# Gate lists of two tokens across the partitions, in a fused Fourier-mixing and expert-lookup kernel

## The chip, the cores and the metric

The kernel runs on one core of one Trainium2 chip. The core's engines are TensorE (PE in the profile, its weight loads PEld), VectorE (DVE), ScalarE (ACT), GpSimd (POOL) and SyncE (SP, which here only issues DMAs). Each runs its own instructions strictly in the order in which they stand; semaphores tie the engines together. The metric is the device time of one execution in microseconds, the median of the runs shown.

## The reference, cut to what matters

```python
xn  = layernorm(x)                                  # 2048 tokens x 512
y   = Real(DFT_seq(DFT_hid(xn)))                    # FNet mixing, as matrices given as inputs
q   = xn @ w_q                                      # 32 heads, 2 x 128
s1, s2 = q1 @ k1.T, q2 @ k2.T                       # 64 keys each
# of each head the two best sums s1[i]+s2[j]: expert index e = 64*i + j, gate g = softmax
act = gelu(sum_d xn[n,d] * u[e,d])                  # 4096 experts
out = sum over heads, k of  g * act * v[e]
result = x + y + out
```

A token has 64 (head, k) entries, each an expert index `e` in 0..4095 and a gate `g`. The kernel computes the gelu for all 4096 experts of a block of 128 tokens with matmuls, and multiplies it by a dense gate matrix that it builds from the lists.

## The kernel before, in words

First comes the Fourier part with the layer norm (to about 90 us of the trace), then the score part (to about 443 us), then the expert part (to the end).

**Score part.** The heads are in 8 chunks (`NCH`), the tokens in 16 tiles of 128. Step n = 16 j + i makes the scores of chunk j and tile i: 12 PE matmuls (`scores`, L799), one ACT eviction (L804), and DVE's MAX8 and FIND_INDEX8 (L807, L811). `routing` turns the top entries into list fields of tile `z`; its small operations go partly to POOL (`ge`). Beside this run preparations of the next chunk's weights (`m_prep`), of the expert tables (`fill_uv`, `fill_far`), and `compare` units: the kernel exploits the symmetry of the DFT matrices, and a `compare` unit loads a piece of those matrices (512 KB) and checks the symmetry. `EARLY` lists the units that run here, at the steps in `at_k`; their loads are issued three steps earlier, the differences are POOL operations (L755, L761), and ACT judges them two steps later (L781). They share three `cx` buffers.

**Expert part.** It works on 14 blocks b of 128 tokens. `u_part(b, cg)`, cg = 0..7, makes the gelu inputs: 48 PE matmuls of 128x128 each (L959), then an ACT gelu (L962). `g_mm(b, tg)` builds the dense gates of 32 tokens: for each 16 tokens DVE writes `L`, a one-hot of the low 7 bits of `e` (128 list entries on the partitions, 16 x 128 columns, L983); for 32 tokens it writes `R`, a one-hot of the high 5 bits (L991), multiplied by the gate (L994). One PE matmul for each token multiplies `L` (weights) with `R` (32 columns) into PSUM tile `g` (L996). The gate is split into a high and a low f16 half, so the 64 entries of a token fill 128 partitions. There are two `L` and two `R` buffers, and two `g` tiles (tag `pg`) of two PSUM banks. `w_part(b, tg)` multiplies `g` by the gelu in place (DVE L1007), ACT makes the f16 high half (L1012) and DVE the low half (L1015, "the subtraction" below); after L1015 the `g` tile is free. `v_part(b, pv, cg)` makes the output: 12 PE matmuls of 128x512 each (L1024), and `finish` adds the rest (L1039) and stores.

PE's order is fixed. In a steady state: the output of block b (cg 0 to 3), `g_mm(b+1, 2)`, the output (cg 4 to 7), `g_mm(b+1, 3)`, `u_part(b+2, 0..3)`, `g_mm(b+2, 0)`, `u_part(b+2, 4..7)`, `g_mm(b+2, 1)`, and on. `g_mm(b, t)` needs the `g` tile that the subtraction two quarters earlier frees.

The lists come to the partitions through `compact`: PE transposes (L698) and one ACT copy (L699) that writes each value twice.

The last two of the 16 token tiles (256 tokens) aren't in blocks. They are done as rows: 128 gathers of u and v rows by POOL (`fetch`, L1050, `BUFS` buffers), a DVE dot product (`dot`, L1066), ACT gelu and scaling (`gain`, L1076 to L1079), and a POOL addition (L1084). `pick` spreads these over the expert part. In the same way `paced` spreads the other `compare` units (`compare`, `compare_r` for rows 0, `compare_w` for the hidden matrix W; here on DVE) and `fit` units, and `after(k, f)` runs f k turns later. `verdict` reduces all checks to flags at cg 4 of the last block.

A scheduler sorts each engine's instructions when the program is built; `follow` and `hold` only bind that order and add no wait on the chip.

Of the kernel before, what the change touches and what calls it, by code (L numbers as in the profile page):

```python
# [10 lines left out]
F16 = mybir.dt.float16  # L11
# [25 lines left out]
def tile_fnet_peer(ctx, tc, x, ca, cb, c5, wt, wf, wr, wq, kt, ut, vn, uv, out):  # L37
# [14 lines left out]
    z_d = dram.tile([NT, P, 3 * P], F16, name="z_d")  # L52
# [40 lines left out]
    EARLY = [*range(8, 24), *range(40, 52)]  # L93
# [462 lines left out]
    def part_b(safe, stS, stP, stE, xt, u_sb, cmp_p):  # L556
# [55 lines left out]
        z = sp.tile([P, NT, 3, 2, 2, H], F16, name="z")  # L612
# [17 lines left out]
        def routing(part, j, vals, idx, t0=0, t1=NT, ge=nc.gpsimd):  # L630
# [20 lines left out]
            elif part == 1:  # L651
# [5 lines left out]
                nc.vector.tensor_copy(zi[:, :, 2, :, 0, hs], g)  # L657
                if not safe and t1 == NT:
                    nc.gpsimd.tensor_copy(gts[:, :, :, hs], g[:, n - NS:])
                nc.vector.tensor_tensor(zi[:, :, 2, :, 1, hs], g, zi[:, :, 2, :, 0, hs], op=ALU.subtract)  # L660
            else:
# [25 lines left out]
                for l in range(2):  # L687
                    for w, v in enumerate((lc, e)):
                        ge.tensor_copy(zi[:, :, w, :, l, hs], v)
# [3 lines left out]
        def compact(b, src, pool, tag):  # L693

            cmp = pool.tile([P, 3, P, 2], F16, tag=tag, name=f"cmp{b}")
            p = pc(f"zt{b}", F16) if b < 2 else psum.tile([P, 512], F16, tag="pb", name=f"zt{b}", bufs=2)
            for w in range(3):
                nc.tensor.transpose(p[:, w * P:(w + 1) * P], src[:, w], ident16)  # L698
            nc.scalar.activation(cmp, p[:, :3 * P].rearrange("p (w n) -> p w n", w=3).unsqueeze(3)  # L699
                                 .to_broadcast([P, 3, P, 2]), AF.Copy)  # L700
            CMP[b] = cmp
# [154 lines left out]
        at_k = [7, 10, *(16 * j + i for j in range(1, 7) for i in (0, 4, 7, 9) if (j, i) != (2, 0)), 112, 122, 125]  # L856
# [8 lines left out]
        for j in range(NCH):  # L865
# [8 lines left out]
            for i in range(NT):  # L874
# [20 lines left out]
                if j + 1 == NCH and i == NT - 1:  # L895
                    for b in range(2):
                        compact(b, z[:, b].rearrange("p w k t h -> p w (k t h)"), cmp_p, f"cmp{b}")
                    nc.sync.dma_start(z_d[2:4].rearrange("i p f -> p i f"),
                                      z[:, 2:4].rearrange("p i a k t h -> p i (a k t h)"))
# [6 lines left out]
        for part in range(3):  # L906
            routing(part, *pend, 4, NT, nc.vector)
        nc.sync.dma_start(z_d[4:].rearrange("i p f -> p i f"),
                          z[:, 4:].rearrange("p i a k t h -> p i (a k t h)"))
# [7 lines left out]
        RS = [lr.tile([P, 32, NC], F16, name=f"R{k}") for k in range(2)]  # L917
# [16 lines left out]
        BUFS = 6  # L934
# [10 lines left out]
        def compact_d(b):  # L945
            zb = bp.tile([P, 3, P], F16, tag="zb", name=f"zb{b}", bufs=1)
# [27 lines left out]
        def g_mm(b, tg, after=None):  # L974
            cmp = CMP[b]
            p = pg(f"g{b}_{tg}")
            def bc(w, t0, t1, n):
                return cmp[:, w, tg * TG + t0:tg * TG + t1, :].unsqueeze(2).to_broadcast([P, t1 - t0, n // 2, 2])

            for hf in range(2):  # L980
                LS.append(LS.pop(0))
                L = LS[-1]
                nc.vector.tensor_tensor(  # L983
                    L.rearrange("p t (l two) -> p t l two", two=2),
                    io_lam.rearrange("p (l two) -> p l two", two=2).unsqueeze(1).to_broadcast([P, 16, P // 2, 2]),
                    bc(0, hf * 16, hf * 16 + 16, P), op=ALU.is_equal)
                if hf == 0:
                    RS.append(RS.pop(0))
                    R = RS[-1]
                    Rv = R.rearrange("p t (c two) -> p t c two", two=2)  # L990
                    nc.vector.tensor_tensor(  # L991
                        Rv, io_c.rearrange("p (c two) -> p c two", two=2).unsqueeze(1)
                        .to_broadcast([P, TG, NC // 2, 2]), bc(1, 0, TG, NC), op=ALU.is_equal)
                    nc.vector.tensor_tensor(Rv, Rv, bc(2, 0, TG, NC), op=ALU.mult)  # L994
                for t in range(16):
                    i = nc.tensor.matmul(p[:, hf, t * NC:(t + 1) * NC], L[:, t, :], R[:, hf * 16 + t, :],  # L996
                                         start=True, stop=True)
                    if after is not None:
                        follow(i.ins, after)
# [109 lines left out]
        def compare_r(n):  # L1109
# [14 lines left out]
            def work():  # L1124
                for ri, odd, e in cls:
                    sgn = (((1, 1, 1), (-1, 1, -1)), ((-1, -1, 1), (1, -1, -1)))[ri][odd]
                    f = (-1 if ri else 1) * sgn[1] * sgn[2]
                    m = ALU.add if ri else ALU.subtract
                    nc.vector.tensor_tensor(tv[e, 1], tv[e, 1], tv[e, 0], op=ALU.subtract if sgn[0] > 0 else ALU.add)
                    nc.vector.tensor_tensor(tv[e, 3], tv[e, 3], tv[e, 2], op=ALU.subtract if f > 0 else ALU.add)  # L1130
                    nc.vector.tensor_tensor(t[e, 0::2, 2:4], t[e, 0::2, 2:4], t[e, 0::2, 0:2], op=m)
                    if odd and ri:
                        nc.vector.tensor_copy(t[e, 2, 0:2], t[e, 0, 0:2])
                    elif odd == ri:
                        nc.vector.memset(t[e, 2, 0:2], 0.0)
                after(2, lambda: nc.scalar.activation(tf[:, P:], tf[:, P:], AF.Abs, accum_out=chk[:, n:n + 1]))

            after(2, work)
# [354 lines left out]
```

## Time and profile before

| | |
|---|---|
| median of 3 runs | 1112.83 us (1112.5 to 1113.57) |
| profiled execution | 1110.31 us, of it 1108.5 us from the first to the last instruction |
| PE busy | 1070.5 us (97%) |
| DVE busy | 963.9 us (87%) |
| ACT busy | 717.3 us (65%) |
| POOL busy | 595.4 us (54%) |

The busy time of an engine is the union of its instructions. A time behind `<-` in brackets is idle time of the engine just before a row, and who ended it. Groups of rows show the shape written and read, the count, the busy time and the mean duration. The durations of consecutive DVE instructions overlap a little; what one costs is the distance from its start to the next start.

### The profile page before, as it was taken

How to read it: one execution, taken by the hardware profiler on the slowest of the kernel's cores; microseconds unless marked ns; L12 is line 12 of the kernel's file. 1: busy time of each engine (PE TensorE's matmuls, PEld its weight loads, DVE VectorE, ACT ScalarE, POOL GpSimd, SP SyncE). 2: the span in 40 equal slices, each digit the busy share in tenths (PEclk: the TensorE clock that was granted, in tenths of full speed). 3: DMA queues.
4: the chain of work that ended last, by engine and by line, in shares of the span. 5: the costliest groups of instructions: out<-in, count | busy, mean ns of one | idle time of the engine just before them, and what ended most of it. 6: DMA issues, size and time to landing. Idle time of an engine off the chain costs nothing. (4 is left out here: it accounts for less than half of the span.)

```text
span 1108.5 us, 28483 instructions
## 1 busy us (share of the span) xinstructions
PE 1070.5 (97%) x11070; PEld 696.6 (63%) x11070; DVE 963.9 (87%) x2748; ACT 717.3 (65%) x1326; POOL 595.4 (54%) x553
## 2 busy tenths in 40 slices
PE   5899999999999999999989999999999999999987
PEld 4355555454544544987675967858667696776933
DVE  6879897979999999987999798999998889998971
ACT  3566657778788767533756766668666776767650
POOL 0013537588797846211646575665575656556431
PEclk9799999999999999999999999999999999999999
DMA  8248153435445331463568667766876667666511
GB/s 326 84 168 288 39 210 99 174 130 208 152 153 197 110 123 65 152 212 92 183 189 248 193 206 244 223 220 191 242 232 214 209 204 252 222 200 200 166 29 51
DMA packets 84936, 196.78 MB, mean 178 GB/s; under 512 B 10770, under 2 KB 27559, under 8 KB 84792
## 3 DMA queue, kind: packets, MB, share of 16 engines
q1 hardware_dynamic: 63898, 123.55, 33.0%
q0 software_dynamic: 20736, 71.31, 21.7%
q8 instruction: 88, 1.44, 0.5%
q14 instruction: 56, 0.46, 0.1%
q10 hardware_dynamic: 158, 0.01, 0.0%
HBM read 177.74 MB, written 17.10 MB: 176 GB/s over the span
## 5 line engine op out<-in xcount | busy, mean ns | idle before, releaser
L799 PE MATMUL s<-m,xq 128*128 128x512 f16 x1536 | 338.9, 379 | 0.0
L959 PE MATMUL z<-xb,u 128*128 128x128 f16 x5376 | 306.4, 220 | 0.0
L959 PEld LDWEIGHTS <-u 128*128 128x128 f16 x5376 | 302.1, 98 | 0.0
L1024 PE MATMUL v<-v,act 128*128 128x512 f16 x1344 | 300.2, 382 | 1.6 <-DVE act L1015 1.6
L1084 POOL TENSOR_TENSOR ov<-ov,ga 128x512 f32<-128x512 f32 x128 | 176.9, 1382 | 206.9 <-ACT ga L1079 173.4
L799 PEld LDWEIGHTS <-xq 128*128 128x128 f16 x1536 | 148.3, 98 | 171.3 <-issue 0.2
L1024 PEld LDWEIGHTS <-act 128*128 128x128 f16 x1344 | 129.6, 98 | 153.2 <-issue 4.5
L983 DVE TENSOR_TENSOR L<-io_lam,cmp 128x2048 f16<-128x2048 f16 x112 | 154.7, 1405 | 31.2 <-PE g L996 31.1
L1050 POOL DMA_INDIRECT ga<-in_uv_dram,eix x128 | 153.4, 1198 | 48.1 <-POOL ov L1084 36.9
L807 DVE MAX8 vals<-ss 128x8 f32<-128x64 f32 x1024 | 152.5, 216 | 14.0 <-ACT ss L804 14.0
L962 ACT ACTIVATE act<-z,scl 128x512 f32<-128x512 f32 x112 | 76.1, 681 | 93.6 <-PE z L959 92.9
L811 DVE FIND_INDEX8 idx<-vals,ss 128x8 uint16<-128x256 f32 x256 | 107.1, 419 | 0.0
L804 ACT ACTIVATE ss<-s,wsc 128x512 f32<-128x512 f32 x112 | 75.5, 680 | 43.1 <-PE s L799 33.8
L1079 ACT ACTIVATE ga<-ga,za 128x512 f32<-128x512 f32 x128 | 92.3, 722 | 10.2 <-ACT za L1077 0.4
L781 ACT ACTIVATE cx<-cx 128x896 f32<-128x896 f32 x64 | 60.6, 947 | 48.7 <-DVE cx L761 36.3
L1066 DVE SCALAR_TENSOR_TENSOR ga<-ga,px 128x512 f32<-128x512 f32 x128 | 85.7, 676 | 0.2
L1012 ACT ACTIVATE act<-g 128x1024 f16<-128x1024 f32 x56 | 73.2, 1308 | 18.2 <-DVE g L1007 18.2
L1007 DVE SCALAR_TENSOR_TENSOR g<-act,scl,g 128x1024 f32<-128x1024 f32 x56 | 71.6, 1279 | 10.7 <-ACT act L962 6.6
L1015 DVE TENSOR_TENSOR act<-g,act 128x1024 f16<-128x1024 f32 x56 | 72.7, 1298 | 6.6 <-ACT act L1012 6.5
L169 POOL TENSOR_TENSOR wq<-wq,wh 128x1024 f16<-128x1024 f32 x26 | 55.5, 2136 | 24.2 <-ACT wq L166 23.7
L996 PE MATMUL g<-R,L 128*128 128x32 f16 x1792 | 53.8, 176 | 13.0 <-DVE act L1015 12.5
L996 PEld LDWEIGHTS <-L 128*128 128x128 f16 x1792 | 51.6, 96 | 21.7 <-DVE act L1015 8.7
(281 smaller groups left out, 1298.4 us busy)
## 6 DMA issues: line engine op xcount, KB each, us to landing
cx<-in_cb_dram SPq DMA_DIRECT2D x50, 448.0 KB
wq<-in_wq_dram SPq DMA_DIRECT2D x32, 512.0 KB
fit<-in_wq_dram SPq DMA_DIRECT2D x28, 512.0 KB
uv<-in_ut_dram SPq DMA_DIRECT2D x16, 512.0 KB
uv<-in_vn_dram SPq DMA_DIRECT2D x16, 512.0 KB
cx<-in_cb_dram SPq DMA_DIRECT2D x28, 224.0 KB
xq<-in_x_dram SPq DMA_DIRECT2D x8, 512.0 KB
xt_d<-xq SPq DMA_DIRECT2D x16, 256.0 KB
```

Of the source, the lines that this page charges most:

```text
L799: mm = nc.tensor.matmul(ps, xt[i][:, l, kd, :], m[:, r, kd, :], start=(n == 0), stop=(n == 3 * KD - 1))
L807: nc.vector.max(vals[:, i, w, :, h], s[:, g, :])
L811: nc.vector.max_index(idx[:, i, w].rearrange("p k h -> p (k h)"), vals[:, i, w, 0:2].rearrange("p k h -> p (k h)"), s[:, w * HC:g + 1, :]. ...
L959: mm = nc.tensor.matmul(p[:, cc * P:(cc + 1) * P], ug[:, l, c % 2, kd, :], xb[:, r, kd, :], start=(n == 0), stop=(n == 3 * KD - 1))
L962: GL[mm.ins.name] = nc.scalar.activation(act[:, cg * 4:cg * 4 + 4, :].rearrange("p c n -> p (c n)"), p, AF.Gelu_apprx_tanh, scale=zsc)
L983: nc.vector.tensor_tensor(L.rearrange("p t (l two) -> p t l two", two=2), io_lam.rearrange("p (l two) -> p l two", two=2).unsqueeze(1).to_ ...
L996: i = nc.tensor.matmul(p[:, hf, t * NC:(t + 1) * NC], L[:, t, :], R[:, hf * 16 + t, :], start=True, stop=True)
L1024: mm = nc.tensor.matmul(pv, w16[:, c, :, l], vg[:, r, c % 2, :], start=(c == 0 and k == 0), stop=(c == NC - 1 and k == 2))
L1050: nc.gpsimd.indirect_dma_start(out=t, out_offset=None, in_=uv, in_offset=bass.IndirectOffsetOnAxis(ap=eix[:, n].rearrange("p k h -> p (k h ...
L1066: nc.vector.scalar_tensor_tensor(t, t, 1.0, T["x"], op0=ALU.mult, op1=ALU.mult, accum_out=T["z", n][:, s:s + 1])
L1079: nc.scalar.activation(t, t, AF.Copy, scale=z)
L1084: T["a"] = nc.gpsimd.tensor_tensor(o, o, t, op=ALU.add)
```

## The change

- A list now has two tokens on the partitions: the 64 entries of an even token on partitions 0 to 63, those of the odd token on 64 to 127. `z` holds five fields of 64 (low bits, high bits, gate high, gate low, low bits again), and `compact` transposes four overlapping pairs of fields (before: three) and writes `cmp` with three ACT copies on 64 partitions each (before: one on 128).
- `g_mm` writes one `L` of 16 x 128 columns for 32 tokens (before: two), one `one_hot` of 16 x 32 columns, and four products of 16 x 32 columns on 64 partitions each, into an `R` that is block-diagonal over the two tokens; its zeros are set once by POOL. PE multiplies 16 times 2: for each pair of tokens the gate's high and low half, with 64 columns, the second added to the first.
- `BUFS` is 5 (before 6).
- `EARLY` has 34 units (before 28): six more `compare` units run in the score part, and more of them in chunks 1, 2 and 7.
- `compare_w` and the work of `compare_r` are cut into pieces in consecutive turns, and are put into the first part of the stream instead of its end (`compare_r`: a little later than before).
- `pick` no longer runs in the last block but one.

DVE's order in the steady state, here while block 8 is put out; `g9_0`, `g9_1` are the `g` tiles of block 9's first two quarters, `act9` its gelu, `cx` a check, `ga` a row. From the first product with `g9_0` to the subtraction that frees it, before:

```order
L1007 SCALAR_TENSOR_TENSOR g9_0_12890<-act9_12546,scl_101,g9_0_12890 128x32x32
L983 TENSOR_TENSOR L1_5793<-io_lam_72,cmp9_12550 128x2048
L1066 SCALAR_TENSOR_TENSOR ga1_18_12838,za1_11802<-ga1_18_12838,px1_11801 128x512
L1007 SCALAR_TENSOR_TENSOR g9_1_13162<-act9_12546,scl_101,g9_1_13162 128x32x32
L755 TENSOR_TENSOR cx53_13201<-cx53_13201 128x256
L755 TENSOR_TENSOR cx53_13201<-cx53_13201 128x512
L991 TENSOR_TENSOR R1_5795<-io_c_73,cmp9_12550 128x1024
L1015 TENSOR_TENSOR act9_12546<-g9_0_12890,act9_12546 128x32x32
```

The same stretch now:

```order
L1016 SCALAR_TENSOR_TENSOR g9_0_13017<-act9_12662,scl_101,g9_0_13017 128x32x32
L1016 SCALAR_TENSOR_TENSOR g9_1_13288<-act9_12662,scl_101,g9_1_13288 128x32x32
L992 TENSOR_TENSOR L1_5836<-io_lam_72,cmp9_12666 128x2048
L1075 SCALAR_TENSOR_TENSOR ga1_18_13064,za1_11919<-ga1_18_13064,px1_11918 128x512
L1001 TENSOR_TENSOR R1_5838<-one_hot_5839,cmp9_12666 64x16x32 x4
L1165 TENSOR_REDUCE sums_92<-cx64_13327 128x1
L1166 TENSOR_TENSOR cx64_13327<-cx64_13327 128x128
L1167 TENSOR_TENSOR cx64_13327<-cx64_13327 128x128
L1226 TENSOR_REDUCE fa_16816<-sums_92 128x1
L1024 TENSOR_TENSOR act9_12662<-g9_0_13017,act9_12662 128x32x32
```

The second product has moved ahead, the whole weight list `L1` and all four products of `R1` stand before the subtraction, and a piece of a W check stands where a `compare` stood.

DVE's order while the last block but one (12) is put out, before, from the first product of block 13 to the subtraction that frees `g13_0`; `cx67` is a W check:

```order
L1007 SCALAR_TENSOR_TENSOR g13_0_16064<-act13_15714,scl_101,g13_0_16064 128x32x32
L1157 SCALAR_TENSOR_TENSOR cx67_16377<-cx67_16377,not0_87 128x128
L1159 SCALAR_TENSOR_TENSOR cx67_16377<-cx67_16377,not0_87 128x128
L1164 TENSOR_TENSOR cx67_16377<-cx67_16377 1x64
L1007 SCALAR_TENSOR_TENSOR g13_1_16340<-act13_15714,scl_101,g13_1_16340 128x32x32
L1165 MEMSET cx67_16377 1x64
L983 TENSOR_TENSOR L0_5792<-io_lam_72,cmp13_15718 128x2048
L1168 SCALAR_TENSOR_TENSOR cx67_16377<-cx67_16377,not0_87 128x256
L1066 SCALAR_TENSOR_TENSOR ga1_61_16011,za1_11802<-ga1_61_16011,px1_11801 128x512
L983 TENSOR_TENSOR L1_5793<-io_lam_72,cmp13_15718 128x2048
L1172 TENSOR_TENSOR cx67_16377<-cx67_16377 128x127
L1015 TENSOR_TENSOR act13_15714<-g13_0_16064,act13_15714 128x32x32
```

And now:

```order
L1016 SCALAR_TENSOR_TENSOR g13_0_16216<-act13_15870,scl_101,g13_0_16216 128x32x32
L1016 SCALAR_TENSOR_TENSOR g13_1_16486<-act13_15870,scl_101,g13_1_16486 128x32x32
L992 TENSOR_TENSOR L1_5836<-io_lam_72,cmp13_15874 128x2048
L1001 TENSOR_TENSOR R1_5838<-one_hot_5839,cmp13_15874 64x16x32 x4
L756 TENSOR_TENSOR cx63_16525<-cx63_16525 128x256
L756 TENSOR_TENSOR cx63_16525<-cx63_16525 128x512
L1024 TENSOR_TENSOR act13_15870<-g13_0_16216,act13_15870 128x32x32
```

The W check and the row are gone from this stretch, one `L` is left of two, and four products and two differences of a `compare` have come in. The core of the diff:

```diff
-    EARLY = [*range(8, 24), *range(40, 52)]
+    EARLY = [*range(8, 24), *range(38, 56)]
...
-            cmp = pool.tile([P, 3, P, 2], F16, tag=tag, name=f"cmp{b}")
+            cmp = pool.tile([P, 4, 64, 2], F16, tag=tag, name=f"cmp{b}")
...
-            for w in range(3):
-                nc.tensor.transpose(p[:, w * P:(w + 1) * P], src[:, w], ident16)
-            nc.scalar.activation(cmp, p[:, :3 * P].rearrange("p (w n) -> p w n", w=3).unsqueeze(3)
-                                 .to_broadcast([P, 3, P, 2]), AF.Copy)
+            for w in range(4):
+                nc.tensor.transpose(p[:, w * P:(w + 1) * P], src[:, w:w + 2].rearrange("p w s -> p (w s)"), ident16)
+            for a, w0, w1, o in ((0, 0, 4, 0), (1, 0, 3, 1), (1, 3, 4, -3)):
+                r = slice(64 * a, 64 * a + 64)
+                nc.scalar.activation(cmp[r, w0 + o:w1 + o], p.rearrange("p (w n a) -> p w a n", w=4, a=2)[r, w0:w1, a]
+                                     .unsqueeze(3).to_broadcast([64, w1 - w0, 64, 2]), AF.Copy)
...
-        at_k = [7, 10, *(16 * j + i for j in range(1, 7) for i in (0, 4, 7, 9) if (j, i) != (2, 0)), 112, 122, 125]
+        at_k = [7, 10, 16, 18, 20, 22, 25, 34, 36, 39, 41, 44, 46,
+                *(16 * j + i for j in range(3, 7) for i in (0, 4, 7, 9)), 112, 115, 118, 122, 125]
...
-        RS = [lr.tile([P, 32, NC], F16, name=f"R{k}") for k in range(2)]
+        RS = [lr.tile([P, 2, 16, 2, NC], F16, name=f"R{k}") for k in range(2)]
+        one_hot = lr.tile([P, 16, NC], F16, name="one_hot")
+        for R in RS:
+            nc.gpsimd.memset(R, 0.0)
...
-        BUFS = 6
+        BUFS = 5
...
+            LS.append(LS.pop(0))
+            RS.append(RS.pop(0))
+            L, R = LS[-1], RS[-1]
+            nc.vector.tensor_tensor(
+                two(L), io_lam.rearrange("p (l two) -> p l two", two=2).unsqueeze(1).to_broadcast([P, 16, P // 2, 2]),
+                bc(0, P), op=ALU.is_equal)
+            nc.vector.tensor_tensor(
+                two(one_hot), io_c.rearrange("p (c two) -> p c two", two=2).unsqueeze(1)
+                .to_broadcast([P, 16, NC // 2, 2]), bc(1, NC), op=ALU.is_equal)
+            for l in range(2):
+                for a in range(2):
+                    r = slice(64 * a, 64 * a + 64)
+                    nc.vector.tensor_tensor(two(R[r, l, :, a]), two(one_hot[r]), bc(2 + l, NC, r), op=ALU.mult)
+            pv = p.rearrange("p h n -> p (h n)")
+            for t in range(16):
+                for l in range(2):
+                    i = nc.tensor.matmul(pv[:, t * 64:(t + 1) * 64], L[:, t, :],
+                                         R[:, l, t].rearrange("p a c -> p (a c)"), start=l == 0, stop=l == 1)
...
-            after(2, work)
+            for k, c in enumerate(cls):
+                after(3 + k, lambda c=c: work(*c))
+            after(8, lambda: nc.scalar.activation(tf[:, P:], tf[:, P:], AF.Abs, accum_out=chk[:, n:n + 1]))
...
-            after(2, lambda: nc.scalar.activation(f, f, AF.Abs, accum_out=chk[:, n + 1:n + 2]))
+            for k, part in enumerate((first, second, third, last)):
+                after(2 + k, part)
+            after(7, lambda: nc.scalar.activation(f, f, AF.Abs, accum_out=chk[:, n + 1:n + 2]))
...
-        units.insert(2, lambda: compare_r(64))
+        for n in range(4):
+            units.insert(3 + 6 * n, units.pop())
+        units.insert(6, lambda: compare_r(64))
...
-                elif b:
-                    pick(mm, cg % 2)
```

116 lines of the change are left out of this document (52 added, 64 removed).

## The prediction

> **What bounds the kernel now.** I read the busy times first, then who PE waited for, then PE's rows in order of time, and then DVE around the waits.
>
> ```profile
> PE 1070.5 (97%) x11070; PEld 696.6 (63%) x11070; DVE 963.9 (87%) x2748; ACT 717.3 (65%) x1326; POOL 595.4 (54%) x553
> ```
> ```profile
> PE g L996 <- DVE act L1015: 12.5, 8, 3.9
> ...
> PE v L1024 <- DVE act L1015: 1.6, 1, 1.6
> PE g L996 <- DVE L L983: 0.3, 1, 0.3
> ```
>
> PE is busy nearly throughout, so a change can save only what PE waits, and costs whatever it adds to PE. The waits view (total us, times, longest) gives the whole stock in the expert part: 12.5 + 1.6 + 0.3 = 14.4 us. All but 0.3 us is for the subtraction L1015, which frees the `g` tile or completes the output's weights. A wait costs a little more than itself:
>
> ```profile
> 561.93 0.97 PE L996 MATMUL g<-R,L 128*128 128x32 f16 x32 [3.10 <-DVE act L1015]
> 562.75 12.51 PE L959 MATMUL z<-xb,u 128*128 128x128 f16 x192
> 575.89 10.88 PE L959 MATMUL z<-xb,u 128*128 128x128 f16 x192
> ...
> 818.07 0.95 PE L996 MATMUL g<-R,L 128*128 128x32 f16 x32 [1.68 <-DVE act L1015]
> 818.87 12.21 PE L1024 MATMUL v<-v,act 128*128 128x512 f16 x48
> 866.08 10.52 PE L1024 MATMUL v<-v,act 128*128 128x512 f16 x48
> ...
> 1063.68 0.95 PE L996 MATMUL g<-R,L 128*128 128x32 f16 x32 [3.92 <-DVE act L1015]
> 1064.48 6.81 PE L1024 MATMUL v<-v,act 128*128 128x512 f16 x23
> 1081.46 20.46 PE L1024 MATMUL v<-v,act 128*128 128x512 f16 x94 [1.60 <-DVE act L1015]
> ```
>
> Behind three waits the same matmuls run slower: 12.51 against 10.88 us, 12.21 against 10.52 us, and 6.81 us for 23 where 10.52 x 23/48 = 5.0 us were due. That is 1.6 + 1.7 + 1.8 = 5.1 us, and with the waits 19.5 us in all. This is the most that the change can gain. DVE is why: of the steady part it is busy nine tenths, and of the rest it spends 31.2 us waiting for PE to give `L` free, with everything else queued behind.
>
> ```profile
> 184.00:227.00 43.00, 43.00 (x284) 20.99 (x282) 37.20 (x199) 32.49 (x49) 30.11 (x30) 1.00 0.43 147
> ...
> 447.00:1050.00 603.00, 594.24 (x8195) 455.19 (x8193) 545.80 (x799) 388.87 (x810) 333.95 (x264) 0.99 0.67 206
> ```
> ```profile
> L983 DVE TENSOR_TENSOR L<-io_lam,cmp 128x2048 f16<-128x2048 f16 x112 | 154.7, 1405 | 31.2 <-PE g L996 31.1
> L991 DVE TENSOR_TENSOR R<-io_c,cmp 128x1024 f16<-128x1024 f16 x56 | 52.9, 944 | 1.1 <-ACT cmp L699 1.0
> L994 DVE TENSOR_TENSOR R<-R,cmp 128x1024 f16<-128x1024 f16 x56 | 48.8, 871 | 1.3
> L755 DVE TENSOR_TENSOR cx<-cx 128x512 f32<-128x512 f32 x27 | 25.7, 951 | 1.3 <-DMA cx<-in_cb_dram 1.3
> L755 DVE TENSOR_TENSOR cx<-cx 128x256 f32<-128x256 f32 x27 | 18.2, 675 | 0.5 <-DMA cx<-in_cb_dram 0.5
> ```
>
> (The windows give, after the length, the busy times of PE, PEld, DVE, ACT, POOL; the first is a piece of the score part, in which PE has no gap at all.)
>
> **What the change adds to PE.** There are as many gate matmuls as before (1792), now with 64 columns. The trace has matmuls of this shape and type in the score part, 24 in a row, and the old shape, 32 in a row:
>
> ```profile
> 140.34 0.22 PE L147 MATMUL m<-sums,wh 128*128 128x64 f16 x2
> ...
> 141.04 1.24 PE L799 MATMUL s<-m,xq 128*128 128x512 f16 x5
> ...
> 463.24 0.95 PE L996 MATMUL g<-R,L 128*128 128x32 f16 x32
> 464.05 8.20 PE L959 MATMUL z<-xb,u 128*128 128x128 f16 x144
> ```
>
> From start to start that is 0.70/24 = 29.2 ns for 64 columns and 0.81/32 = 25.3 ns for 32: 1792 x 3.9 ns = +6.9 us, all on the path, as PE is the bound. The fourth transpose of `compact` costs 10.88/192 = 0.057 us in each of 14 blocks: +0.8 us. Together +7.7 us, certain as far as any term here.
>
> **What it takes from DVE.** From start to start an operation on 2048 columns costs 1.14 us (868.25 below to the row at 869.39 that follows it), one on 1024 columns 872.73 - 872.13 = 0.60 us, so one on 512 columns about 0.60 - 0.54/2 = 0.33 us by that slope.
>
> ```profile
> 865.48 0.69 ACT L962 ACTIVATE act<-z,scl 128x512 f32<-128x512 f32 x1 [0.77 <-PE z L959]
> ...
> 867.06 1.28 DVE L1007 SCALAR_TENSOR_TENSOR g<-act,scl,g 128x1024 f32<-128x1024 f32 x1
> 868.25 1.21 DVE L983 TENSOR_TENSOR L<-io_lam,cmp 128x2048 f16<-128x2048 f16 x1
> 869.39 0.68 DVE L1066 SCALAR_TENSOR_TENSOR ga<-ga,px 128x512 f32<-128x512 f32 x1
> ...
> 872.13 0.68 DVE L991 TENSOR_TENSOR R<-io_c,cmp 128x1024 f16<-128x1024 f16 x1
> 872.73 1.30 DVE L1015 TENSOR_TENSOR act<-g,act 128x1024 f16<-128x1024 f32 x1
> ...
> 876.44 0.95 PE L996 MATMUL g<-R,L 128*128 128x32 f16 x32
> ```
>
> The four products alternate between partitions 0 and 64. The nearest rows are those of `compare_r`, whose pieces start at different partitions:
>
> ```profile
> 559.80 0.43 DVE L1129 TENSOR_TENSOR cx_r<-cx_r 4x256 f32<-4x256 f32 x1
> 560.15 0.41 DVE L1130 TENSOR_TENSOR cx_r<-cx_r 4x256 f32<-4x256 f32 x1
> 560.60 1.28 DVE L1015 TENSOR_TENSOR act<-g,act 128x1024 f16<-128x1024 f32 x1
> ```
>
> On the same partitions the second starts 0.35 us behind the first, though the first lasts 0.43 us; the operation that goes back to partition 0 comes 0.45 us behind one that lasts 0.41 us. So I add 0.10 us to each product: 0.43 us. [...] Without it the saving would be twice as large: 39 us against 16 us.
>
> A quarter of a block cost 2 x 1.14 + 2 x 0.60 = 3.48 us and costs 1.14 + 0.33 + 4 x 0.43 = 3.19 us: 56 x 0.29 = 16 us less. Six `compare` units leave DVE: 6 x (0.951 + 0.675) = 10 us. And `L` is no longer taken twice per quarter, so the 31.2 us of blocked time shrink. DVE's load falls by about 26 us in 603, and its order loosens. None of that is on the path by itself; it decides what is left of the 19.5 us.
>
> **What is left of the waits.** The last one, 1.60 us at 1081.46, stays: in the new order the subtraction for the last quarter still stands behind the last block's L1039, which waits for PE. The 0.3 us at the first `g` stays too. For the wait of 3.92 us look at the second pair of orders: before, a W check stood between, and PE waited for the chain from the first product; now the chain is 2 x 1.19 (867.06 to 868.25) + 1.14 + 4 x 0.43 + two differences (0.675 + 0.951) + 1.30 = 8.2 us. PE needs it 39 matmuls, some 8.5 us, after the gelu's matmuls end, and the gelu itself takes ACT 0.69 us and stands behind other ACT work: 0.4 to 2.6 us are late, I take 1.2 us. In the steady blocks the same chain is 2 x 1.19 + 1.14 + 0.6 + 1.72 + about 0.9 for the piece of check + 1.30 = 8.0 us. It can start when the gelu is done (865.48 + 0.69 = 866.17) and would end at 874.2; PE comes at 876.44, 2.2 us later. A collision with a POOL addition takes from that (an `R` lasts 0.944 us on average, 0.68 us undisturbed). The three other quarters gain more room, because the second product stands earlier. I leave 2.5 us for all eleven steady blocks. Sum left: 1.6 + 0.3 + 1.2 + 2.5 = 5.6 us, so the gain is 19.5 - 5.6 = 13.9 us.
>
> **What I cost at nothing.** Six more `compare` units in the score part are POOL and ACT work beside an ungapped PE:
>
> ```profile
> L755 POOL TENSOR_TENSOR cx<-cx 128x512 f32<-128x512 f32 x20 | 25.5, 1274 | 2.8 <-DMA cx<-in_cb_dram 2.8
> L755 POOL TENSOR_TENSOR cx<-cx 128x256 f32<-128x256 f32 x20 | 14.6, 731 | 0.0
> L761 POOL TENSOR_TENSOR cx<-cx 128x128 f32<-128x128 f32 x24 | 10.9, 456 | 8.3 <-issue 7.0
> ```
>
> Each takes POOL 2.5 us. Chunk 2 (the window 184 to 227 us) gets three more: 30.1 + 7.4 = 37.5 of 43 us. `routing` queues behind them on POOL, and DVE behind `routing`; four eviction tiles and four PSUM tiles, 8 steps of PE, stand between DVE and PE. Their loads queue on SP for three buffers and are needed three steps later. `compact`'s three ACT copies on half the partitions instead of one are half a microsecond more per block on an engine two thirds busy. POOL's two fills of `R` fall into its idle time before the first gather. Five row buffers:
>
> ```profile
> DMA to landing us min/median/max: 4.1/5.1/10.7
> ```
>
> One buffer less takes one row's spacing, 4.4 us (128 rows over some 560 us), from a lead of about 20 us; a gather lands in 5.1 us, at worst 10.7 us. The rows that `pick` no longer does in the last block but one go to the last, where DVE has little to do, and the flags have room:
>
> ```profile
> 1096.11 0.15 DVE L1231 TENSOR_TENSOR flags<-flag,flag 1x1 int32<-1x1 int32 x1
> 1101.96 0.75 DVE L1039 SCALAR_TENSOR_TENSOR y<-v,scl,y 128x512 f32<-128x512 f32 x1 [5.71 <-PE v L1024]
> ```
>
> **Sum.** +7.7 - 13.9 = -6.2 us on the profiled execution's 1110.31 us, 1104.1 us. The runs shown are 2.5 us above it, so I put the difference on their median: 1112.83 - 6.2 = 1106.6 us.
>
> **Rivals.** (1) Slower: the waits move to `g_mm(b, 2)`. There the new order is worse: `L` and four products stand ahead of the subtraction, and the room of 2.2 us is what two collisions with POOL (1.27 us each where DVE meets the start of an addition) would use up. At 1 us per block, 11 us are left beside 3.1 us: 19.5 - 14.1 = 5.4 us of gain, 1115.1 us; with as much waiting as before, 1112.83 + 7.7 = 1120.5 us. It decides from 11.8 us of waits on, 0.8 us per block. Against it: the quoted block has 2.2 us. (2) Matmuls of 64 columns cost no more than of 32, when what limits both is not the columns: the 6.9 us vanish, 1099.7 us. [...] (3) Rows come late with five buffers, DVE stands in front of them, and PE waits some 4 us more: 1110.6 us. (4) The denser checks hold POOL or SP in chunks 1, 2 and 7, and PE gets gaps or the first `g` is late by about 4 us: 1110.6 us.
>
> **Chances.** Forecast 0.64; (1) 0.18; (2) 0.04; (3) 0.07; (4) 0.07. What this kernel's measurement can tell from no change is about 0.2%, 2.2 us. The forecast and (2) are faster, except 0.04 in the forecast's upper tail; (3) and (4) lie around 1110.6 us, a third of each faster; (1) is slower but for 0.03. Faster 0.64 + 0.04 - 0.04 + 0.05 = 0.69, same 0.04 + 0.07 + 0.03 = 0.14, slower 0.17. The lower end is all waits gone but the 1.6 and 0.3 us, 1112.83 + 7.7 - 17.6 = 1102.9 us, less a little for the bounds of the matmul's cost: 1101.5 us. The upper end takes in the first half of (1): 1116 us. The likeliest case alone spans 1102 to 1110 us.
>
> **What the changed profile would show.** Gate matmuls with 64 columns 29 ns apart; `L` 56 times and no longer with 31 us of idle time before it; products of 0.4 us; PE's waits for the subtraction about 5 us in all, hardly any before the last two blocks, and no slow stretch behind them; PE ungapped in the score part. I am wrong if the waits before `g_mm(b, 2)` add up to over 10 us, if the products cost much more than 0.43 us, or if PE waits for `R`, a row or a load.

## The result, and the profile after

The changed kernel takes 1120.66 us (median; 1119.61 to 1123.72) beside 1112.66 us for the kernel before: a ratio of 1.0089 (95% interval 1.0069 to 1.0108), 8.0 us slower where 6 us faster was forecast. The profiled execution has a span of 1118.3 us, 9.8 us more than before.

The busy times of the page and the waits of PE (total us, times, longest):

```profile
PE 1075.3 (96%) x11084; PEld 703.3 (63%) x11084; DVE 936.7 (84%) x2842; ACT 722.0 (65%) x1342; POOL 594.3 (53%) x566
```
```profile
PE g L1005 <- DVE act L1024: 12.6, 10, 2.5
...
PE s L800 <- ACT ss L805: 4.2, 2, 3.0
PE v L1033 <- DVE y L1048: 0.8, 1, 0.8
PE v L1033 <- DVE act L1024: 0.6, 1, 0.6
```

DVE is busy 27 us less, as worked out (26 us), and PE waits for DVE in the expert part as long as before: 12.6 + 0.8 + 0.6 = 14.0 us (0.8 us of it for the output, L1048) beside 14.4 us (0.3 us of it for `L`). A wait that was not there before stands in the score part, 4.2 us.

The costs per instruction came out as forecast. From PE's timeline, a quarter's 32 gate matmuls:

```profile
463.35 1.10 PE L1005 MATMUL g<-R,L 128*128 128x64 f16 x32
464.28 0.89 PE L964 MATMUL z<-xb,u 128*128 128x128 f16 x13
...
826.77 1.09 PE L1005 MATMUL g<-R,L 128*128 128x64 f16 x32 [2.47 <-DVE act L1024]
827.70 10.52 PE L1033 MATMUL v<-v,act 128*128 128x512 f16 x48
```

They start 0.93/32 = 29.1 ns apart with 64 columns, against 25.1 ns with 32 before. The last two rows show that the matmuls behind a wait of 2.47 us run at full speed (48 in 10.52 us): no slow stretch is left in the expert part. The clock shows the same: behind the wait at 818.07 us in the kernel before the granted clock was 0.50 from 819.04 to 822.45 us, and here it is 1.00 from 822.40 to 832.64 us.

The 9.8 us of the profiled span by stage, from the same rows before and after:

| stage | us | what |
|---|---|---|
| up to the score part | +0.4 | |
| score part | +6.4 | 1.4 at the start of chunk 3 and 4.8 in chunk 7: waits of 1.27 and 2.98 us, and 1.7 us of slow matmuls behind the second (granted clock 0.50 from 429.87 to 433.28 us); 0.1 for two more transposes |
| first `g` (456.6, now 463.3) to PE's end | +2.6 | matmuls 1792 x 4.0 ns = +7.2, the other transposes +0.7, waits -0.4, slow stretches -5.0 |
| store at the end | +0.4 | |

### Where the score part lost its time

The start of chunk 3, after:

```profile
233.08 1.95 POOL L756 TENSOR_TENSOR cx<-cx 128x512 f32<-128x512 f32 x2
...
235.52 0.32 POOL L645 TENSOR_TENSOR c<-vals 128x64 f32<-128x64 f32 x1
...
237.86 0.26 ACT L653 ACTIVATE c<-c 128x64 f32<-128x64 f32 x1 [6.24 <-POOL c L650]
...
240.63 1.67 PE L800 MATMUL s<-m,xq 128*128 128x512 f16 x7 [1.27 <-ACT ss L805]
```

Here `routing` begins on POOL, behind the differences of the added units of chunk 2: L645 starts at 235.52 us, in the kernel before at 230.91 us. ACT stands 6.24 us at the exponential L653 (2.96 us before), and the eviction that PE needs stands behind it.

Chunk 7 in the timeline of all engines, after, and below it `routing`'s first operation in the kernel before:

```profile
423.13 2.13 POOL L608 TENSOR_TENSOR v<-uv,v 128x1024 f16<-128x1024 f32 x1
423.40 1.89 DVE L645 TENSOR_TENSOR c<-vals 128x16 f32<-128x16 f32 x1
...
425.21 2.00 POOL L756 TENSOR_TENSOR cx<-cx 128x256 f32<-128x256 f32 x2
...
427.55 0.27 DVE L650 TENSOR_TENSOR c<-c,c 128x16 f32<-128x16 f32 x1
...
427.91 0.21 ACT L653 ACTIVATE c<-c 128x16 f32<-128x16 f32 x1 [6.92 <-DVE c L650]
428.04 0.94 ACT L782 ACTIVATE cx<-cx 128x896 f32<-128x896 f32 x1
...
428.97 0.67 ACT L805 ACTIVATE ss<-s,wsc 128x512 f32<-128x512 f32 x1
...
429.69 0.87 PE L800 MATMUL s<-m,xq 128*128 128x512 f16 x2 [2.98 <-ACT ss L805]
```
```profile
421.78 0.16 DVE L645 TENSOR_TENSOR c<-vals 128x16 f32<-128x16 f32 x1
```

Here `routing` runs on DVE. Its first operation L645 takes 1.89 us beside a POOL operation of `fill_uv` (423.13 us), and L647 and L648 (0.70 and 1.22 us, before 0.17 us each) meet the POOL differences of the unit at step 118. From L645 to the end of L650 it takes 4.4 us, before 1.0 us. ACT stands 6.92 us at the exponential L653, which needs them. Behind it on ACT are the judging of a compare unit (0.94 us) and then the eviction that PE waits for. So in chunk 3 `routing` is late in POOL's queue, in chunk 7 POOL holds up its operations on DVE, and both times ACT's queue carries the delay to PE.

### Where the waits of the expert part come from

The block of tokens 10, from PE's arrival at the output of block 9 to `g_mm(10, 2)`, after:

```profile
923.94 2.48 DVE L1016 SCALAR_TENSOR_TENSOR g<-act,scl,g 128x1024 f32<-128x1024 f32 x2 [2.08 <-ACT act L967]
923.96 10.52 PE L1033 MATMUL v<-v,act 128*128 128x512 f16 x48
...
926.25 1.27 POOL L1093 TENSOR_TENSOR ov<-ov,ga 128x512 f32<-128x512 f32 x1 [1.24 <-ACT ga L1088]
926.33 2.27 DVE L992 TENSOR_TENSOR L<-io_lam,cmp 128x2048 f16<-128x2048 f16 x1
927.30 1.30 ACT L1021 ACTIVATE act<-g 128x1024 f16<-128x1024 f32 x1
...
928.52 5.03 DVE L1001 TENSOR_TENSOR R<-one_hot,cmp 64x512 f16<-64x512 f16 x4
929.46 1.28 POOL L1093 TENSOR_TENSOR ov<-ov,ga 128x512 f32<-128x512 f32 x1
...
931.99 1.27 POOL L1093 TENSOR_TENSOR ov<-ov,ga 128x512 f32<-128x512 f32 x1
...
935.12 1.27 DVE L1024 TENSOR_TENSOR act<-g,act 128x1024 f16<-128x1024 f32 x1
...
936.45 0.74 PE L1005 MATMUL g<-R,L 128*128 128x64 f16 x20 [1.97 <-DVE act L1024]
```

The high half (ACT, L1021) is ready at 928.60, and the subtraction starts at 935.12. Ahead of it on DVE stand `L` and the four products of the quarter after this one, which PE needs only at 948, and then two differences of a check and a row (1.5 us). `L` meets one POOL addition (2.27 us instead of 1.21), the products meet two (5.03 us instead of 1.71).

### The profile page after: what moved, and what is told of

Same layout as the page of the kernel before. It is cut to its first block, busy times and chain, and to the rows that moved or that the text cites. A ratio compares the mean times of both kernels' runs of the same rounds, so it can differ in the third digit from the quotient of the medians.

```text
span 1118.3 us, 28675 instructions
## 1 busy us (share of the span) xinstructions
PE 1075.3 (96%) x11084; PEld 703.3 (63%) x11084; DVE 936.7 (84%) x2842; ACT 722.0 (65%) x1342; POOL 594.3 (53%) x566
## 5 line engine op out<-in xcount | busy, mean ns | idle before, releaser
L1033 PE MATMUL v<-v,act 128*128 128x512 f16 x1344 | 296.8, 379 | 1.4 <-DVE y L1048 0.8
L1093 POOL TENSOR_TENSOR ov<-ov,ga 128x512 f32<-128x512 f32 x128 | 170.7, 1334 | 232.1 <-ACT ga L1088 193.3
L1059 POOL DMA_INDIRECT ga<-in_uv_dram,eix x128 | 141.9, 1109 | 48.6 <-POOL ov L1093 36.3
L1001 DVE TENSOR_TENSOR R<-one_hot,cmp 64x512 f16<-64x512 f16 x224 | 138.7, 619 | 14.5 <-PE g L1005 11.8
L1016 DVE SCALAR_TENSOR_TENSOR g<-act,scl,g 128x1024 f32<-128x1024 f32 x56 | 71.0, 1282 | 38.5 <-ACT act L967 26.8
L1021 ACT ACTIVATE act<-g 128x1024 f16<-128x1024 f32 x56 | 73.1, 1308 | 21.8 <-DVE g L1016 21.3
L1075 DVE SCALAR_TENSOR_TENSOR ga<-ga,px 128x512 f32<-128x512 f32 x128 | 86.0, 678 | 0.5
L992 DVE TENSOR_TENSOR L<-io_lam,cmp 128x2048 f16<-128x2048 f16 x56 | 73.5, 1313 | 2.5 <-PE g L1005 2.5
L1005 PE MATMUL g<-R,L 128*128 128x64 f16 x1792 | 61.2, 193 | 12.6 <-DVE act L1024 12.6
L1005 PEld LDWEIGHTS <-L 128*128 128x128 f16 x1792 | 58.7, 98 | 20.2 <-issue 14.8
```

The lines of the kernel that those rows point to most:

```text
L992: nc.vector.tensor_tensor(two(L), io_lam.rearrange("p (l two) -> p l two", two=2).unsqueeze(1).to_broadcast([P, 16, P // 2, 2]), bc(0, P), ...
L1001: nc.vector.tensor_tensor(two(R[r, l, :, a]), two(one_hot[r]), bc(2 + l, NC, r), op=ALU.mult)
L1005: i = nc.tensor.matmul(pv[:, t * 64:(t + 1) * 64], L[:, t, :], R[:, l, t].rearrange("p a c -> p (a c)"), start=l == 0, stop=l == 1)
L1033: mm = nc.tensor.matmul(pv, w16[:, c, :, l], vg[:, r, c % 2, :], start=(c == 0 and k == 0), stop=(c == NC - 1 and k == 2))
L1059: nc.gpsimd.indirect_dma_start(out=t, out_offset=None, in_=uv, in_offset=bass.IndirectOffsetOnAxis(ap=eix[:, n].rearrange("p k h -> p (k h ...
L1075: nc.vector.scalar_tensor_tensor(t, t, 1.0, T["x"], op0=ALU.mult, op1=ALU.mult, accum_out=T["z", n][:, s:s + 1])
```

## The experiments

Ratios are to the kernel before on the same chip, with the 95% interval.

| kernel | median us | ratio | first `g` | waits for the subtraction |
|---|---|---|---|---|
| changed | 1120.66 | 1.0089 (1.0069 to 1.0108) | 463.3 | 12.6 + 1.4 |
| units28 | 1120.87 | 1.0067 (1.0048 to 1.0086) | 457.4 | 16.2 + 1.4 |
| no_row_adds | 1108.47 | 0.9953 (0.9934 to 0.9971) | 462.4 | 0.5 + 1.4 |
| order_rule | 1112.36 | 0.9987 (0.9977 to 0.9997) | 464.3 | 3.9 + 1.4 |
| lists_only | 1127.99 | 1.0129 (1.0112 to 1.0146) | 458.4 | 18.4 + 1.6 |
| checks_only | 1119.19 | 1.0054 (1.0031 to 1.0078) | 465.3 | 11.4 + 1.4 |
| rule_spread | 1110.41 | 0.9975 (0.9958 to 0.9993) | 463.7 | 3.9 + 0.8 |
| checks_spread | 1115.21 | 1.0007 (0.9985 to 1.0029) | 464.7 | 10.1 + 0.8 |
| rule_halves | 1109.14 | 0.9962 (0.9946 to 0.9977) | 463.0 | 2.2 + 1.4 |
| rule_units28 | 1102.29 | 0.9928 (0.9909 to 0.9947) | 456.6 | 2.7 + 0.8 |
| rule_units32 | 1104.12 | 0.9942 (0.9923 to 0.9962) | 460.9 | 0.8 + 0.8 |
| rule_units30 | 1102.52 | 0.9906 (0.9888 to 0.9924) | 457.4 | 1.4 + 0.8 |
| old_lists28 | 1106.67 | 0.9946 (0.9926 to 0.9965) | 456.5 | 8.7 + 0.8 |

(The last column is the wait before `g` and, behind the plus, in the last block; there the wait for y, which stands ahead of the subtraction, is counted in. Waits for `L` or `R`, 1.0 us at most, and waits whose end the profile puts down to nothing, 2.6 us at most, in checks_only, are not. The kernels ran on several chips. The kernel before took 1113.4 us beside units28 to lists_only, 1112.8 us beside checks_only to rule_halves, 1109.5 us beside rule_units28 and rule_units32, and 1113.0 us beside the last two, so between these groups the ratios compare better than the times.)

### The six units moved back

```diff
-    EARLY = [*range(8, 24), *range(38, 56)]
+    EARLY = [*range(8, 24), *range(40, 52)]
...
-        at_k = [7, 10, 16, 18, 20, 22, 25, 34, 36, 39, 41, 44, 46,
-                *(16 * j + i for j in range(3, 7) for i in (0, 4, 7, 9)), 112, 115, 118, 122, 125]
+        at_k = [7, 10, *(16 * j + i for j in range(1, 7) for i in (0, 4, 7, 9) if (j, i) != (2, 0)), 112, 122, 125]
```

> The changed kernel with the 28 early compare units and their old steps; the other six run on DVE in the expert part again. Theory (the six units cost the score part 6.3 us: POOL reaches routing later, ACT stands in its queue at the exponential L653 and the evictions behind it are late): PE's two gaps of 1.27 and 2.98 us in the score part are gone and the first g starts at about 457 us instead of 463.3; the expert part gets 10 us more of DVE work, which costs 0 to 4 us; about 1115.5 us, between 1114 and 1118.5. Rival (the new list layout in routing delays the score part): the gaps stay, 1120.7 us or more.

Both gaps of the score part are gone and the first `g` starts 5.9 us earlier, so the six units were the cause, not the layout of the lists. But the time is the same, the rival's number without its mechanism: PE's waits for the subtraction grow to 16.2 us, the longest 5.0 us, and the expert part is 7 us longer, more than the 0 to 4 us expected: 4.7 us more of waits, and 1.7 us of slow matmuls behind the longest.

```profile
PE g L1004 <- DVE act L1023: 16.2, 11, 5.0
...
PE v L1032 <- DVE y L1047: 0.8, 1, 0.8
```

In this order of DVE, 10 us of its work were worth as much as what the score part paid.

### No additions on POOL

```diff
             for t in T.pop("t"):
-                T["a"] = nc.gpsimd.tensor_tensor(o, o, t, op=ALU.add)
+                if n == 0 and s == 0 or s == N - 1:
+                    T["a"] = nc.gpsimd.tensor_tensor(o, o, t, op=ALU.add)
                 fetch()
```

> The changed kernel without the POOL additions of the gathered rows (all but the first and the last of each token tile are left out; the result of the 256 tokens done as rows is not computed). Theory (in the expert part the products meet POOL additions, some 1.15 us each, and hold up the subtraction behind them): the products fall from 0.62 to about 0.43 us on average, PE's waits for the subtraction from 12.6 to under 4 us, with the slow stretches behind them 9 to 13 us less: 1108 to 1112 us. Rival (the order alone is too long, with or without POOL): at least 8 us of waits stay, 1116 us or more.

This kernel leaves out 125 of the 128 additions. The waits before `g` all but vanish, and no product is held up any more: 0.418 us on average. Those two rows and the products' group in the changed kernel:

```profile
PE g L1005 <- DVE act L1024: 0.5, 2, 0.3
```
```profile
L1001 DVE TENSOR_TENSOR R<-one_hot,cmp 64x512 f16<-64x512 f16 x224 | 93.6, 418 | 24.1 <-PE g L1005 17.3 <-remote 4.0
```
```profile
L1001 DVE TENSOR_TENSOR R<-one_hot,cmp 64x512 f16<-64x512 f16 x224 | 138.7, 619 | 14.5 <-PE g L1005 11.8
```

DVE does the same work here in the same order, but for one `L`. So the collisions with POOL are one half of the cause.

### A rule for DVE's order

```diff
-                nc.vector.tensor_tensor(w16[..., 1], w, w16[..., 0], op=ALU.subtract)
+                SUB[b, tg] = nc.vector.tensor_tensor(w16[..., 1], w, w16[..., 0], op=ALU.subtract)
...
-                    nc.vector.tensor_tensor(two(R[r, l, :, a]), two(one_hot[r]), bc(2 + l, NC, r), op=ALU.mult)
+                    i = nc.vector.tensor_tensor(two(R[r, l, :, a]), two(one_hot[r]), bc(2 + l, NC, r), op=ALU.mult)
+                    k = divmod(4 * b + tg - 3, 4)
+                    if k in SUB:
+                        follow(i.ins, SUB[k])
```

> The changed kernel with one rule for DVE's order: the four products of a quarter stand behind the subtraction of three quarters earlier, which the g matmuls of the quarter before need. Theory (the waits come from L and products ahead of the subtraction): PE's waits for the subtraction fall from 12.6 to 2 to 5 us, 1109 to 1114 us, the score part unchanged. Rival (DVE is late by its load, whatever the order): the waits stay above 9 us, 1118 us or more; or PE waits for the products instead, as many us as were saved.

The waits fall to 3.9 us, with POOL's additions as before; PE does not wait for the products instead (in rule_spread below it does once, 0.7 us).

```profile
PE s L800 <- ACT ss L805: 4.3, 2, 3.0
PE g L1009 <- DVE act L1028: 3.9, 3, 1.7
```

The products still meet POOL: 41 of the 336 operations that make `L` and `R` are over 0.3 us longer than their median, 47 us in all, beside 48 of 336 and 52 us in the changed kernel. They now meet it where nobody waits. `L` still stands ahead of the subtraction; of the theory only the products have moved. So the order is the other half: the waits need both.

### The change in two halves

Lists alone: the hunks of the diff that make and use the lists, and `BUFS = 5`. Checks alone: all other hunks (`EARLY`, `at_k`, the pieces, the order of the units, `pick`).

> The kernel before with the two-token lists (and five row buffers, without which they do not fit) alone: early units, checks and rows as before. Theory: the score part is as before (first g at about 457 us, no gap); in the expert part the wider matmuls cost 7.7 us, the waits stay or grow since the checks come in one piece: 1115 to 1120 us, I take 1117. Rival (the lists by themselves save the waits, and only the moved checks cost): 1108 to 1111 us.

Slower than expected, by 11 us. The score part is as before (first `g` at 458.4, of whose delay 1.7 us are already there at the start of chunk 1). In the expert part PE waits more than ever, 18.4 us before `g`, and the wider matmuls and two slow stretches (at 829.58 and 1078.75 us, granted clock 0.50 for 3.41 us each) come on top.

```profile
PE g L1004 <- DVE act L1023: 18.4, 12, 4.2
...
PE v L1032 <- DVE act L1023: 1.6, 1, 1.6
```

> The kernel before with everything but the lists: 34 early units, checks in pieces, W among the first blocks, no rows in the last block but one; old lists, six row buffers. Theory (the score part loses 6.3 us, and the expert part gains since DVE has 10 us less to do and short pieces stand ahead of the subtraction): the two gaps of 1.3 and 3.0 us in the score part are there, the waits for the subtraction fall from 14.1 us to 4 to 8 us; 1106 to 1112 us, I take 1108. If effects only add up, the changed kernel less the lists alone, 1120.7 - 1128.0 + 1113.4 = 1106.1 us. Rival (the moved checks are what makes the changed kernel slow): 1117 us or more.

This is the rival's number: 1119.2 us. The score part's loss is there (5.2 us of waits), and the waits for the subtraction stay at 11.4 us. But the rival's reason is only half right, as old_lists28 below shows. The two halves do not add up: 14.6 us and 6.4 us slower alone, 8.0 us together.

### Other places for the six units

```diff
-        at_k = [7, 10, 16, 18, 20, 22, 25, 34, 36, 39, 41, 44, 46,
-                *(16 * j + i for j in range(3, 7) for i in (0, 4, 7, 9)), 112, 115, 118, 122, 125]
+        at_k = [7, 10, 12, 14, 16, 18, 20, 22, 25, 28, 30, 34, 36, 39, 41,
+                *(16 * j + i for j in range(3, 7) for i in (0, 4, 7, 9)), 112, 122, 125]
...
             i = nc.vector.scalar_tensor_tensor(y, pv, osc, y, op0=ALU.mult, op1=ALU.add)
+            if b + 2 == NB:
+                follow(i.ins, SUB[b + 1, 3])
```

> The kernel with the order rule (1112.4 us), and the six added units in chunks 0 and 1 (steps 12, 14, 28, 30 among them) instead of at steps 44, 46, 115 and 118; and y of the last block but one behind the last subtraction. Theory (the loss of the score part belongs to the steps where the units meet routing): first g at about 458 us, no gap in the score part, the two waits of 0.8 and 0.6 us in the last block gone; 1112.4 - 6 - 1.5 = 1105 us, between 1103 and 1108. Rival (34 units anywhere in the score part cost the same): new gaps, 1110 us or more.

> The kernel before with old lists and the moved checks (as in checks_only), the added units at the steps of rule_spread, and the same order at the last block. Theory (the wider matmuls and the split products cost more than they gave, the rest of the change is a gain once its units stand clear of routing): 7 us less than checks_only, 1099 to 1105 us, the fastest of all. Rival (the lists are needed for the gain): as slow as rule_spread or slower, 1105 us or more.

Both rivals' times: 1110.4 us and 1115.2 us. The gaps in chunks 3 and 7 are gone, and there is a new one in chunk 1. POOL of rule_spread:

```profile
132.26 2.13 POOL L169 TENSOR_TENSOR wq<-wq,wh 128x1024 f16<-128x1024 f32 x1
145.59 1.94 POOL L756 TENSOR_TENSOR cx<-cx 128x512 f32<-128x512 f32 x2 [11.20 <-DMA cx<-in_cb_dram]
147.48 0.32 POOL L650 TENSOR_TENSOR c<-c,c 128x64 f32<-128x64 f32 x1
```
```profile
148.72 1.44 PE L800 MATMUL s<-m,xq 128*128 128x512 f16 x3 [4.09 <-ACT ss L805]
```

A load was late: POOL stood 11.2 us at it, and `routing` (L650) stood behind on POOL, the exponential and the evictions behind that on ACT. The buffers were not the reason, as ACT had judged the two units ahead by 126.4 us. In SP's queue the two loads, at 137.81 and 138.81 us, stand behind two stores `y_d<-u` of the Fourier part, whose issue took 5.71 and 5.26 us. The changed kernel has the same two stores (5.74 and 5.26 us), but the unit whose load stands behind them there is worked on later, and POOL does not wait for it. The reordered end of the last block but one took away 0.6 us of the 1.4 us.

### Products by halves

```diff
-            for l in range(2):
-                for a in range(2):
+            for a in range(2):
+                for l in range(2):
```

> The kernel with the order rule, the four products in the order of the partition halves (both of the lower half, then both of the upper) instead of alternating. Theory (0.10 us is paid at each change of the starting partition): a product that is followed by one of the same half has 0.33 us from start to start, one at a change 0.43 us; DVE gets about 56 x 2 x 0.1 = 11 us less to do, which is off the path: 1110 to 1112.5 us beside 1112.4. Rival (the 0.43 us belong to the form of the product): 0.43 us everywhere, no change.

Four undisturbed products and the operation behind them, in this kernel and in the changed one:

```profile
928.23 1.52 DVE L1002 TENSOR_TENSOR R<-one_hot,cmp 64x512 f16<-64x512 f16 x4
929.78 1.29 DVE L1020 SCALAR_TENSOR_TENSOR g<-act,scl,g 128x1024 f32<-128x1024 f32 x1
```
```profile
1069.67 1.71 DVE L1001 TENSOR_TENSOR R<-one_hot,cmp 64x512 f16<-64x512 f16 x4
1071.40 1.03 DVE L756 TENSOR_TENSOR cx<-cx 128x256 f32<-128x256 f32 x2
```

1.55 us against 1.73 us: in another group of four the starts are 0.33 and 0.34 us apart within a half and 0.42 us at the change, where the changed kernel has 0.42 or 0.43 us everywhere. So the 0.10 us belong to the change of the starting partition. 56 quarters x 0.18 us are 10 us less for DVE. The time is 1 us under the expected range: the waits before `g` fell from 3.9 to 2.2 us, and 1.2 us were already there at the start of chunk 1; the two kernels also ran on different chips.

### Rule and units together

> The kernel of rule_halves (1109.1 us) with the 28 early units and their old steps, and y of the last block but one behind the last subtraction. Theory (with the rule DVE has room, so that six more compare units in the expert part cost little, and the score part gets its 6 us back): first g at about 457 us, waits for the subtraction 2 to 5 us, 1109.1 - 5.9 - 0.8 + 1 to 3 = 1102.5 to 1106 us, I take 1104. Rival (10 us more on DVE cost the expert part 5.5 us in any order, as they did without the rule): 1108 us.

> As rule_units28, but with 32 early units: the changed kernel's steps without 115 and 118. Theory (those two units cost the score part 4.8 us in chunk 7, the other four 1.4 us at the start of chunk 3): the gap of 3.0 us is gone, that of 1.3 us stays; 1109.1 - 4.8 - 0.8 + 0 to 1 = 1103.5 to 1104.5 us. Rival (the gap in chunk 7 comes from elsewhere): it stays, 1108 us.

> As rule_units28, but with 30 early units: of the changed kernel's steps those of chunk 1 (16, 18, 20, 22, 25) and chunk 2 without 44 and 46, and chunk 7 as before. Theory (only a unit whose load or whose work meets routing costs the score part): no gap in the score part, DVE has 3 us less to do in the expert part: 1101 to 1102.5 us, at or just under rule_units28. Rival (each unit moved into the score part costs about 1 us of PE time): 1104 us.

All three came out as the theory had them, the first 0.2 us under its range (it was worked out from a time on another chip; by the ratios rule_units28 is 0.3% faster than rule_halves, by the profiled spans 7.2 us): 1102.3, 1104.1 and 1102.5 us, 0.6 to 0.9% faster than the kernel before, and faster than the changed one by more. PE's waits in the score and the expert part of rule_units28, and of rule_units32:

```profile
PE g L1008 <- DVE act L1027: 2.7, 2, 2.1
PE v L1036 <- DVE y L1051: 0.8, 1, 0.8
```
```profile
PE s L800 <- ACT ss L805: 1.2, 1, 1.2
...
PE v L1037 <- DVE y L1052: 0.8, 1, 0.8
PE g L1009 <- DVE act L1028: 0.8, 1, 0.8
```

Without the units at 115 and 118 the gap of 3.0 us is gone and that of 1.2 us (chunk 3) stays, which goes with the units at 44 and 46 (rule_units30). With the rule, six units more on DVE in the expert part cost nothing that shows: in the profiles PE needs 637.7 us from the first `g` to its end with 28 early units and 638.3 us with 34 (rule_halves; 0.6 us of it is the wait that the new place of y takes away), and the first `g` comes 6.4 us earlier.

### Old lists with all the rest

> The kernel before with old lists and 28 early units at their old steps, the checks in pieces, W among the first blocks, no rows in the last block but one, and y of the last block but one behind the last subtraction: what rule_units28 has beside the new lists. Theory (with the old lists DVE stands in front of L until PE gives it free, and the subtraction behind it stays late whatever the checks do): no gap in the score part, 10 us or more of waits for the subtraction, 1110 to 1115 us. Rival (the lists are not needed, the pieces alone make the gain): 1105 us or less.

Neither: 1106.7 us, faster than before and slower than with the new lists. On the same chip rule_units30 took 1100.8 to 1104.0 us, this kernel 1101.7 to 1110.5 us. Its profiled execution was one of its fastest (1102.2 us), and waits 8.7 us for the subtraction; DVE stands 26.7 us in front of `L`:

```profile
PE g L997 <- DVE act L1016: 8.7, 6, 2.9
...
PE v L1025 <- DVE y L1040: 0.8, 1, 0.8
```
```profile
L984 DVE TENSOR_TENSOR L<-io_lam,cmp 128x2048 f16<-128x2048 f16 x112 | 153.8, 1399 | 26.7 <-PE g L997 26.7
```

So most of the gain over the kernel before does not need the new lists; which of the pieces, the order of the units, the later rows and the order at the end brings it was not separated. The lists with the rule (and two more early units) are worth some 4 us of the median on that chip and a narrower spread. In the two profiled executions, one each, they are worth nothing: from the first `g` to PE's end it takes 637.1 us in rule_units30 and 637.4 us here, where 6.4 us more of waits and a slow stretch of 1.7 us stand against 8 us less of matmuls and transposes. The difference of the medians goes with the granted clock, which is 0.994 where this kernel took 1101.7 and 1102.2 us and 0.986 where it took 1110.5 us, and 0.990 to 0.995 in rule_units30. The medians of checks_only and this kernel lie 12.5 us apart, their profiled executions 17.1 us: 8.8 us is the earlier first `g`, 5.5 us is waits of PE behind it, and the rest stays open.

## Why the prediction was wrong

**Held.** PE as the bound. The wider matmuls and transposes: 7.7 us forecast, 7.2 + 0.7 = 7.9 us measured. The product at 0.43 us undisturbed, with 0.10 us for the change of the half. DVE's load: 26 us less forecast, 27 us measured. The 31.2 us in front of `L` fell to 2.5 us, but DVE now waits 11.8 us for PE in front of `R` and 11.4 us in front of the product L1016 (2.0 us before), so most of the blocked time has only moved. The last block: 1.6 us forecast, 0.8 + 0.6 us measured. Five row buffers: DVE waits 0.5 us in all before the row products.

**Right by luck.** The slow stretches: 5.1 us forecast to go, 5.0 us gone from the expert part. The forecast let them go with the waits, but ten waits of up to 2.5 us before `g` stayed, and units28 and lists_only, with the same lists, have one and two slow stretches again. Rival (1)'s 1120.5 us for "as much waiting as before" is also met by chance: it left the slow stretches in place and the score part alone, and 5.0 us less and 6.2 us more nearly cancel.

**Wrong: "I leave 2.5 us for all eleven steady blocks".** 12.6 us stayed, 7.5 us of them before `g_mm(b, 2)` in six blocks and 5.2 us before `g_mm(b, 0)` and `g_mm(b, 1)`. The step took one block of the kernel before, with 2.2 us of room, as typical, and let a collision "take from that". A quarter meets 48/56 = 0.9 collisions of 1.1 us, and the room is that of a quarter without any. "The three other quarters gain more room" failed too, by the 5.2 us in four of their waits. For the 7.5 us the mechanism was that of rival (1), which stood at 0.18: `L` and the four products ahead of the subtraction. Its condition, two collisions with POOL in one chain, was written down and not weighed against a count of the collisions in the kernel before, which had 45 on 224 such operations, 46 us. The wait of 3.92 us in the last block but one, for which 1.2 us were left, is gone altogether.

**Wrong: "What I cost at nothing", the six units.** They cost 6.2 us. The share of POOL's time in the chunk (37.5 of 43 us) was no argument: what counted was that `routing` stood behind a unit in POOL's order (chunk 3, 1.4 us) or was held up on DVE beside POOL's operations (chunk 7, 4.8 us), and the count of "8 steps of PE" between DVE and PE looked at the wrong queue. ACT stood at L653 and the evictions behind it. Rival (4) named the effect, with a price of 4 us and a chance of 0.07. The kernel before already showed ACT standing at L653 for 5.2 us at the longest:

```profile
ACT c L653 <- POOL c L650: 15.3, 6, 4.9
ACT c L653 <- DVE c L650: 8.4, 2, 5.2
```

**Refuted.** Rivals (2) and (3): the matmul costs 29.1 ns, and no row came late.

With the two mis-sized terms the sum comes out: -6.2 + (14.0 - 5.6) + 6.2 = +8.4 us, and 8.0 us were measured between the medians (9.8 us between the profiled executions).

## What to carry to other kernels

A lighter engine helps only where its order lets it (here 27 us less on DVE left PE 14.0 us of waits beside 14.4 us): before counting a saving on an in-order engine as room, list what stands between the operation that the bound engine waits for and the moment when its input is ready, and whether its neighbours can be moved behind it. Work that goes to a half idle engine is free only if nothing urgent stands behind it, in its own queue or in the queue of an engine that waits for it, and if it holds up no urgent operation of another engine (here 1.4 us in chunk 3 and 4.8 us in chunk 7). Count collisions between two engines by the operations that cause them, not by the load of the one that suffers (here 45 and 48 beside 128 additions, with DVE 27 us less busy).

## What the runs showed of the hardware

The collisions between DVE and POOL hardly depend on DVE's load or its split into operations: 45 on 224 operations before (46 us over their medians), 48 on 336 after (52 us), 37 to 48 in the other kernels (39 to 52 us) with 128 POOL additions in each, and none in no_row_adds, which has 3. Two operations of the changed kernel that read PSUM were not longer beside the same additions: L1016 takes 1.29 us at most (median 1.28), L1075 (its second operand is in PSUM) 0.69 us (median 0.68).

A wait of PE is followed by slow matmuls in some places and not in others, and the wait's length does not tell which: behind 1.68 us before (818 us) 48 matmuls took 12.21 us, behind 2.47 us after (827 us) 10.52 us. In these two kernels each slow stretch behind such a wait is 3.41 us at a granted clock of 0.50, so it costs 1.7 us. In the kernel before they begin at 563.04, 819.04 and 1064.80 us, in the changed kernel one begins at 429.87 us. Why a wait is followed by one or not was not tested.
